# A 2-D FFT filter beside a gated MLP on one core: filter weights read in runs of four, the spectrum read from PSUM with a stride

## The chip, the cores and the metric

The kernel runs on one core of a Trainium2 chip. The metric is device time in microseconds (us) of one execution, measured outside the profiler. The profile of one execution stands beside it; its "span" runs from the first to the last instruction that it records. Engines are called TensorE (PE; its weight loads are PEld), VectorE (DVE), ScalarE (ACT), GpSimd (POOL) and SyncE (SP, which issues most of the DMAs here).

## What is computed

With x of 2048 x 640, in bf16:

```python
xn = layernorm(x)                              # over the 640 columns
X  = rfft2(xn); X = X * (w_r + 1j * w_i)       # 2048 x 321 complex filter
A  = irfft2(X)
B  = ((x_n @ w_gate) * (x_n @ w_up)) @ w_down  # 640 -> 1536 -> 640, x_n = xn
return x + A + B
```

All inputs and the output are bf16. The filter weights w_r and w_i are 2048 x 321 each.

## The kernel before, in words

The kernel is written as tasks (a few instructions of one engine each) with data dependencies, a duration that is written into the code, and a priority. A planner in the same file places the tasks on the engines by these durations before anything runs, and gives each engine one fixed list of instructions with its semaphore waits. So the order of the work follows from the tasks, their dependencies and the written durations, and not from what happens on the chip.

The stages overlap. First x is loaded, normalised and transposed (xn^T for the MLP). The 640 columns are split as 10 x 64: VectorE does the length-10 transforms by additions and multiplications (tasks S1 to S5, lines 833 to 873), TensorE the rest. The rows, 2048 = 32 x 64, are transformed in two matmul steps (R, line 884, and then D and C). The MLP's gate and up matmuls (GU, line 923; ten matmuls of 256 columns for most tasks) are scattered between all of this as filling for TensorE; ScalarE copies their results from PSUM (line 704), and VectorE multiplies gate and up (H, line 938).

The filter stage is a loop over 16 groups t of 128 spectrum rows each (line 947). One round has these tasks:

- four loads of filter weights into one of four buffers of `v_w` (line 698 by way of `dma`, each 64 rows x 321 columns, on SP's queue); a buffer is free when the multiplication four rounds earlier has read it.
- D (line 964): five matmuls finish the column transform; eD copies it from PSUM as bf16.
- C (lines 985 to 988): four matmuls of 321 columns make the real and imaginary spectrum in two neighbouring PSUM banks, 321 fp32 columns in each. The first 256 columns of a bank are four blocks k of 64 columns. Such a block holds two halves h of 32 columns m. Column (k, h, m) is frequency 10m + k + 1 for h = 0 and 10m + 9 - k for h = 1. The last 65 columns are the frequencies that are multiples of 5.
- WM (lines 992 to 1006): VectorE multiplies the spectrum in PSUM by the weights in SBUF. For each half h and each of w_r and w_i there is one TENSOR_TENSOR of 256 elements (line 1000), 2 banks x 4 k x 32 m with m innermost; then one of 260 elements for the last 65 columns (line 1003). The products are fp32 in `v_p`.
- CB (lines 1018 to 1022): four VectorE instructions add and subtract the products into the new real and imaginary parts, as bf16, in `v_y`; in `v_y` each block k holds three pieces of 64: the negated sum, the difference, the sum.
- NG (lines 1028 to 1030): ScalarE writes the negated sum (256 elements) and two small copies.
- IA (lines 1041 and 1042): ten matmuls, two for each of five blocks, go back along the rows; the 128 columns of a load of TensorE weights are two neighbouring pieces of `v_y`. eIA copies the result from PSUM.

After the 16 rounds come the inverse column transforms (I, line 1068, and V1 to V5 on VectorE), the accumulation with w_down (ACC, line 1141: 12 matmuls of 320 columns for each half of 128 output rows), one last matmul that adds A to it (line 1149), and the addition of x on VectorE (line 1156).

Of the kernel before, what the change touches and what calls it, by code (L numbers as in the profile page):

```python
# [495 lines left out]
_ACTF = mybir.ActivationFunctionType  # L496
_OP = AluOpType
# [13 lines left out]
def _d_mm(n):  # L511
    return max(n, 64) / 2.4 + 2.5
# [32 lines left out]
def _build(nc, A_x, A_w_r, A_w_i, B_w_gate, B_w_up, B_w_down, out, opts=None):  # L545
# [3 lines left out]
    with es:  # L549
# [68 lines left out]
        def V(name):  # L618
            off, sz = lay[name]
            return arena[:, off: off + sz]  # L620
# [8 lines left out]
        v_w = V("W").rearrange("p (r w l) -> p r w l", r=_NW, w=2)  # L629
# [5 lines left out]
        v_ti = V("TI").rearrange("p (t c n) -> p t c n", t=16, c=2)  # L635
# [14 lines left out]
        v_p = V("P").bitcast(_F32).rearrange("p (r w c l) -> p r w c l", r=2, w=2, c=2)  # L650
        v_y = V("Y").rearrange("p (r n) -> p r n", r=2)
# [37 lines left out]
        def bank_of(t):  # L689
            return t.units[1]  # L690
# [256 lines left out]
        for t in range(16):  # L947
            pq = 10.0 + 0.05 * t
            ar = t % 3
            r2 = t % 2  # L950
            wr = t % _NW
            for w_ in range(2):
                for h in range(2):
                    k2 = int(_rows(t, 0, h, 0))
                    dma("ld_w%d_%d_%d" % (t, w_, h), v_w[64 * h:64 * h + 64, wr, w_, 0:321], wvs[w_][:, k2, :],
                        64 * 642, [(b_w, ("r", 4 * wr + 2 * w_ + h, 4 * wr + 2 * w_ + h + 1))], prio=9.5 + 0.05 * t,
                        semkey=("w", wr), after=[wpad])

            def em_d(c, t=t):
                bk = bank_of(c.t)  # L960
                ins = None
                for k in range(5):
                    n = 128 if k < 4 else 130
                    ins = c.e.matmul(psflat[:, bk * 512 + k * 128: bk * 512 + k * 128 + n], v_uq[:, k, t, :],
                                     v_fd[:, k * 128: k * 128 + n], start=True, stop=True)
                return ins
            td = T("D_%d" % t, "pe", 5 * _d_mm(128), em_d, reads=[(b_u, None), (b_fd, None)],
                   prio=pq, bank="pair", cls="a")

            def em_ed(c, td=td, ar=ar):  # L970
                bk = bank_of(td)
                src = psflat[:, bk * 512: bk * 512 + 642]
                dst = v_a[:, ar, :].rearrange("p (c n) -> p c n", c=2)
                copy_on(c, dst[:, :, 0:256].rearrange("p c (k m) -> p k c m", k=4),
                        src[:, 0:512].rearrange("p (k c m) -> p k c m", k=4, c=2))
                return copy_on(c, dst[:, :, 256:321], src[:, 512:642].rearrange("p (c m) -> p c m", c=2))
            ed = T("eD_%d" % t, ("act", "dve"), {"dve": _d_dve_psum(512) + _d_dve_psum(130), "act": _d_act(512) + _d_act(130)}, em_ed,
                   writes=[(b_a, ("r", ar, ar + 1))], prio=pq - 0.001, frees=td)
            hold(td, ed)

            def em_c(c, t=t, ar=ar):
                bk = bank_of(c.t)
                a_r = v_a[:, ar, 0:_LP]
                a_i = v_a[:, ar, 324:324 + _LP]
                c.e.matmul(ps[:, bk, 0:_LP], v_tf[:, t, 0, :], a_r, start=True, stop=False)
                c.e.matmul(ps[:, bk + 1, 0:_LP], v_tf[:, t, 0, :], a_i, start=True, stop=False)
                c.e.matmul(ps[:, bk, 0:_LP], v_tf[:, t, 1, :], a_i, start=False, stop=True)
                return c.e.matmul(ps[:, bk + 1, 0:_LP], v_tf[:, t, 2, :], a_r, start=False, stop=True)
            tc = T("C_%d" % t, "pe", 4 * _d_mm(_LP), em_c, reads=[(b_a, ("r", ar, ar + 1)), (b_tf, ("t", t, t + 1))],
                   prio=pq, bank="pair", cls="a")  # L990

            def em_wm(c, tc=tc, r2=r2, wr=wr):
                bk = bank_of(tc)
                ins = None
                for h in range(2):
                    xh = ps[:, bk:bk + 2, 0:256].rearrange("p c (k h m) -> p h c k m", k=4, h=2)[:, h]
                    wv = v_w[:, wr, :, 0:320].rearrange("p w (m k) -> p w k m", k=10)
                    wv = wv[:, :, 1:5, :] if h == 0 else wv[:, :, 9:5:-1, :]
                    for w in range(2):
                        c.e.tensor_tensor(  # L1000
                            v_p[:, r2, w, :, 0:256].rearrange("p c (k h m) -> p h c k m", k=4, h=2)[:, h], xh,
                            wv[:, w].unsqueeze(1).to_broadcast([128, 2, 4, 32]), _OP.mult)
                ins = c.e.tensor_tensor(  # L1003
                    v_p[:, r2, :, :, 256:321], ps[:, bk:bk + 2, 256:321].unsqueeze(1).to_broadcast([128, 2, 2, 65]),
                    v_w[:, wr, :, 0:321:5].unsqueeze(2).to_broadcast([128, 2, 2, 65]), _OP.mult)
                return ins
            wm = T("WM_%d" % t, "dve", 4 * _d_dve_psum(256) + _d_dve_psum(260), em_wm,
                   reads=[(b_w, ("r", 4 * wr, 4 * wr + 4)), (b_wp, None)],
                   writes=[(b_p, ("r", r2, r2 + 1))], prio=pq - 0.001, frees=tc)
            hold(tc, wm)  # L1010

            def em_cb(c, r2=r2):
                p00, p01, p10, p11 = (v_p[:, r2, 0, 0], v_p[:, r2, 0, 1], v_p[:, r2, 1, 0], v_p[:, r2, 1, 1])

                def k4(v):
                    return v[:, 0:256].rearrange("p (k m) -> p k m", k=4)
                ym = v_y[:, r2, 0:768].rearrange("p (k s m) -> p k s m", k=4, s=3)
                c.e.tensor_tensor(ym[:, :, 2, :], k4(p01), k4(p10), _OP.add)  # L1018
                c.e.scalar_tensor_tensor(v_y[:, r2, 896:961], p01[:, 256:321], -1.0, p10[:, 256:321], _OP.mult,
                                         _OP.subtract)  # L1020
                c.e.tensor_tensor(v_y[:, r2, 768:833], p00[:, 256:321], p11[:, 256:321], _OP.subtract)
                return c.e.tensor_tensor(ym[:, :, 1, :], k4(p00), k4(p11), _OP.subtract)  # L1022
            T("CB_%d" % t, "dve", 2 * _d_dve(256) + 2 * _d_dve(65), em_cb,
              reads=[(b_p, ("r", r2, r2 + 1))], writes=[(b_y, ("r", 2 * r2, 2 * r2 + 1))], prio=pq - 0.001)

            def em_ng(c, r2=r2):
                ym = v_y[:, r2, 0:768].rearrange("p (k s m) -> p k s m", k=4, s=3)
                c.e.activation(ym[:, :, 0, :], ym[:, :, 2, :], _ACTF.Copy, scale=-1.0)  # L1028
                c.e.activation(v_y[:, r2, 833:896], v_y[:, r2, 897:960], _ACTF.Copy, scale=-1.0)
                return c.e.activation(v_y[:, r2, 961:1024], v_y[:, r2, 769:832], _ACTF.Copy)  # L1030
            T("NG_%d" % t, "act", _d_act(256) + 2 * _d_act(63), em_ng,
              reads=[(b_y, ("r", 2 * r2, 2 * r2 + 1))], writes=[(b_y, ("r", 2 * r2 + 1, 2 * r2 + 2))],
              prio=pq - 0.001)

            def em_ia(c, t=t, r2=r2):
                bk = bank_of(c.t)
                ins = None
                for k in range(5):
                    o1, o2 = (192 * k + 64, 192 * k) if k < 4 else (768, 896)
                    dst = psflat[:, bk * 512 + k * 128: bk * 512 + (k + 1) * 128]  # L1040
                    c.e.matmul(dst, v_y[:, r2, o1:o1 + 128], v_ti[:, t, 0, :], start=True, stop=False)  # L1041
                    ins = c.e.matmul(dst, v_y[:, r2, o2:o2 + 128], v_ti[:, t, 1, :], start=False, stop=True)  # L1042
                return ins
            ia = T("IA_%d" % t, "pe", 10 * _d_mm(128), em_ia, reads=[(b_y, ("r", 2 * r2, 2 * r2 + 2)), (b_ti, None)],
                   prio=pq, bank="pair", cls="a")

            def em_eia(c, ia=ia, t=t):
                bk = bank_of(ia)
                src = psflat[:, bk * 512: bk * 512 + 640].rearrange("p (k a m) -> p k a m", k=5, a=16)
                return copy_on(c, v_z2w[:, :, :, t, :], src)  # L1050
            eia = T("eIA_%d" % t, ("act", "dve"), {"dve": _d_dve_psum(640), "act": _d_act(640)}, em_eia,
                    writes=[(b_z2, ("t", t, t + 1))], prio=pq - 0.001, frees=ia)
            hold(ia, eia)
# [3 lines left out]
        for a in range(16):  # L1057
            pa = 19.0 + 0.05 * a
            pc = 41.0 + 0.05 * a
            r2 = a % 2  # L1060
# [185 lines left out]
```

## Time and profile before

| what | value |
|---|---|
| time, median of 3 runs (lowest to highest) | 224.96 us (224.48 to 225.21) |
| the profiled execution | 224.85 us |
| its span | 222.7 us |
| granted TensorE clock | 1.0 over the whole span |
| TensorE busy | 210.5 us, 2116 matmuls |
| VectorE busy | 197.7 us, 535 instructions |
| ScalarE busy | 129.4 us, 292 instructions |
| the 64 multiplications of line 1000 | 613 ns each, first start 89.3 us, last start 146.4 us |

A row of a group of instructions reads: line, engine, operation, what is written <- what is read, partitions x elements with type, xcount | busy time, mean ns of one | idle time of the engine just before them. Neighbouring rows of one engine overlap in the trace (an instruction is recorded until its last write, when the next has begun), so the time that an instruction takes in a full queue is read from start to start. In the rows of the timeline the columns are start, length, engine, line, operation, shape, count. In the rows of the waits they are who waited <- for whom: us in total, times, longest.

### The profile page before, as it was taken

The numbers are of one execution on the slowest core, as the hardware profiler recorded it, in microseconds if no ns is written. First come the engines' busy times: TensorE is split into PE (matmuls) and PEld (weight loads), VectorE is DVE, ScalarE is ACT, GpSimd is POOL, SyncE is SP. The second block draws the span as 40 slices with busy tenths as digits, with TensorE's granted clock in tenths as the row PEclk, the third lists the DMA queues.
The fourth block names the chain that finished last, engine by engine and source line by source line (L and its number), as shares of the span: only waits on it lengthen the run. The fifth ranks groups of instructions, "written<-read, shape, count | busy, mean of one in ns | idle before, by whom it ended". The sixth has DMA issues, their size and how long they took to land.

```text
span 222.7 us, 5325 instructions
## 1 busy us (share of the span) xinstructions
PE 210.5 (95%) x2116; PEld 173.0 (78%) x2116; DVE 197.7 (89%) x535; ACT 129.4 (58%) x292; POOL 0.2 (0%) x4
## 2 busy tenths in 40 slices
PE   8999999999999999889898989989999999999995
PEld 8989899988789988667676767779876767777773
DVE  3699999999999992999999999976999999999631
ACT  2575999999998658668677876587522012200000
POOL 0000000000000000000000000000000000000000
PEclk9999999999999999999999999999999999999999
DMA  7999990000000000012121211008622223332311
GB/s 196 306 345 393 405 204 9 0 3 0 1 3 0 3 0 3 21 40 53 39 49 44 52 41 30 3 0 258 215 60 61 74 72 93 92 99 78 116 46 44
DMA packets 22184, 19.78 MB, mean 89 GB/s; under 512 B 2192, under 2 KB 21264, under 8 KB 21904
## 3 DMA queue, kind: packets, MB, share of 16 engines
q1 hardware_dynamic: 20048, 18.37, 27.6%
q10 hardware_dynamic: 2112, 1.08, 1.9%
q8 instruction: 16, 0.26, 0.5%
q14 instruction: 8, 0.07, 0.1%
HBM read 16.82 MB, written 2.62 MB: 87 GB/s over the span
## 4 chain that ended last, share of the span: by engine, by line
PE 50%; DVE 42%; DMA 2%; ACT 2%; issue 1%; SPq 0%; DVEq 0%
PE ps L923 24%; PE ps L1141 20%; DVE arena L1000 14%; DVE arena L938 3%; DVE arena L1018 3%; DVE arena L1003 2%; DMA arena<-in_A_x_dram 2%; DVE arena L1022 2%; PE ps L1068 2%; ACT arena L704 2%; PE ps L1149 2%; PE ps L813 1%; PE ps L884 1%; DVE arena L798 1%; DVE arena L837 1%
## 5 line engine op out<-in xcount | busy, mean ns | idle before, releaser
L704 ACT ACTIVATE arena<-ps 128x512 bf16<-128x512 f32 (+5 forms) x200 | 106.6, 582 | 48.7 <-PE ps L1068 26.1
L923 PE MATMUL ps<-arena 128*128 128x256 bf16 (+1 forms) x1080 | 113.6, 261 | 3.3 <-DVE arena L1003 2.7
L923 PEld LDWEIGHTS ps<-arena 128*128 128x128 bf16 x1080 | 93.3, 98 | 14.7 <-DVE arena L1003 3.7
L1141 PE MATMUL ps<-arena 128*128 128x320 bf16 x384 | 56.7, 299 | 0.0
L1141 PEld LDWEIGHTS ps<-arena 128*128 128x128 bf16 x384 | 37.3, 98 | 14.2
L1000 DVE TENSOR_TENSOR arena<-ps,arena 128x256 f32<-128x256 f32 x64 | 35.0, 613 | 0.0
L938 DVE TENSOR_TENSOR arena<-arena 128x512 bf16<-128x512 bf16 (+1 forms) x54 | 20.9, 389 | 7.3 <-ACT arena L704 7.2
L1156 DVE TENSOR_TENSOR arena<-ps,arena 128x320 bf16<-128x320 f32 x32 | 15.5, 486 | 8.1 <-PE ps L1149 8.1
L1041 PE MATMUL ps<-arena 128*128 128x128 bf16 x80 | 10.7, 219 | 2.7 <-DVE arena L1003 1.9
L1041 PEld LDWEIGHTS ps<-arena 128*128 128x128 bf16 x80 | 7.6, 97 | 5.9 <-ACT arena L704 3.1
L1028 ACT ACTIVATE arena<-arena 128x256 bf16<-128x256 bf16 x16 | 6.6, 416 | 9.4 <-DVE arena L1022 9.4
L1042 PE MATMUL ps<-arena 128*128 128x128 bf16 x80 | 10.6, 219 | 0.0
L1149 PE MATMUL ps<-arena 128*128 128x320 bf16 x32 | 9.6, 299 | 0.0
L837 DVE TENSOR_TENSOR arena<-arena 128x384 f32<-128x384 bf16 x16 | 8.9, 554 | 0.0
L1042 PEld LDWEIGHTS ps<-arena 128*128 128x128 bf16 x80 | 7.8, 98 | 0.0
L764 DVE BATCH_NORM_STATS2 arena<-arena 128x6 f32<-128x320 bf16 x8 | 3.9, 490 | 3.8 <-DMA arena<-in_A_x_dram 3.6
L1003 DVE TENSOR_TENSOR arena<-ps,arena 128x260 f32<-128x260 f32 x16 | 7.1, 441 | 0.0
L1018 DVE TENSOR_TENSOR arena<-arena 128x256 bf16<-128x256 f32 x16 | 6.8, 425 | 0.2
L813 PE MATMUL ps<-arena 128*128 128x128 bf16 x80 | 6.3, 219 | 0.6 <-ACT arena L704 0.4
L757 ACT ACTIVATE arena<-arena 128x640 bf16<-128x640 bf16 x8 | 6.8, 846 | 0.0
L1022 DVE TENSOR_TENSOR arena<-arena 128x256 bf16<-128x256 f32 x16 | 6.8, 422 | 0.0
L838 DVE TENSOR_TENSOR arena<-arena 128x256 f32<-128x256 bf16 x16 | 6.7, 421 | 0.0
(71 smaller groups left out, 224.6 us busy)
## 6 DMA issues: line engine op xcount, KB each, us to landing
arena<-in_A_x_dram SPq DMA_DIRECT2D x20, 160.0 KB, 2.9
out_dram<-arena SPq DMA_DIRECT2D x32, 80.0 KB, 1.6
arena<-in_B_w_down_dram SPq DMA_DIRECT2D x1, 1920.0 KB, 9.0
arena<-c_tf SPq DMA_DIRECT2D x4, 384.0 KB, 11.6
arena<-in_A_w_r_dram SPq DMA_DIRECT2D x32, 40.1 KB, 2.3
arena<-in_A_w_i_dram SPq DMA_DIRECT2D x32, 40.1 KB, 2.3
arena<-in_B_w_gate_dram SPq DMA_DIRECT2D x4, 320.0 KB, 7.8
arena<-in_A_x_dram SPq DMA_DIRECT2D x1, 1280.0 KB, 12.1
```

The costliest lines, as they stand in the source:

```text
L704: return c.e.activation(dst, src, _ACTF.Copy)
L923: ins = c.e.matmul(ps[:, bk, w * n:(w + 1) * n], v_gw[:, w, j, ft, :], v_xt[:, j, rows], start=(j == 0), stop=(j == 4))
L938: return c.e.tensor_tensor(v_ht[:, ft0:ft0 + 2, rows], v_gbf[:, rr, :, 0:n], v_gbf[:, rr, :, n:2 * n], _OP.mult)
L1000: c.e.tensor_tensor(v_p[:, r2, w, :, 0:256].rearrange("p c (k h m) -> p h c k m", k=4, h=2)[:, h], xh, wv[:, w].unsqueeze(1).to_broadcast( ...
L1003: ins = c.e.tensor_tensor(v_p[:, r2, :, :, 256:321], ps[:, bk:bk + 2, 256:321].unsqueeze(1).to_broadcast([128, 2, 2, 65]), v_w[:, wr, :, 0 ...
L1018: c.e.tensor_tensor(ym[:, :, 2, :], k4(p01), k4(p10), _OP.add)
L1022: return c.e.tensor_tensor(ym[:, :, 1, :], k4(p00), k4(p11), _OP.subtract)
L1041: c.e.matmul(dst, v_y[:, r2, o1:o1 + 128], v_ti[:, t, 0, :], start=True, stop=False)
L1042: ins = c.e.matmul(dst, v_y[:, r2, o2:o2 + 128], v_ti[:, t, 1, :], start=False, stop=True)
L1141: ins = c.e.matmul(ps[:, bk, 0:320], v_ht[:, ft, a * 128:(a + 1) * 128], v_wd[:, ft, sl3], start=(ft == 0), stop=False)
L1149: return c.e.matmul(ps[:, bank_of(ag2), 0:320], v_sm[:, 2, :], v_v[:, a, sl3], start=False, stop=True)
L1156: return c.e.tensor_tensor(v_out[:, a % 2, sl3], ps[:, bk, 0:320], v_xr[:, xs, sl3], _OP.add)
```

## The change

Only access patterns change, in four tasks of the filter round. Each engine has the same instructions with the same numbers of elements in the same order with the same waits in both kernels; the durations written into the tasks are the same too.

- WM: the four multiplications of line 1000 run over 2 banks x 32 m x 4 k, with k innermost. The weights of one m are then four neighbours in SBUF (backwards for h = 1), and the next m is ten elements on. The spectrum in PSUM is read with k innermost, which is a step of 64 fp32 columns (256 bytes) from element to element. The products are written in order, for h = 0 in columns 0 to 127 and for h = 1 in columns 128 to 255, index 4m + k in each.
- CB and NG: the same sums in the new order, as one run of 256 elements each instead of four runs of 64. `v_y` holds the negated sum in 0 to 255, the difference in 256 to 511, the sum in 512 to 767.
- IA: for the first four blocks the 128 columns of the TensorE weights are taken from `v_y` with a step of four elements (8 bytes), where they were neighbours. The fifth block stays as it was.

```diff
                     xh = ps[:, bk:bk + 2, 0:256].rearrange("p c (k h m) -> p h c k m", k=4, h=2)[:, h]
-                    wv = v_w[:, wr, :, 0:320].rearrange("p w (m k) -> p w k m", k=10)
-                    wv = wv[:, :, 1:5, :] if h == 0 else wv[:, :, 9:5:-1, :]
+                    wv = v_w[:, wr, :, 0:320].rearrange("p w (m k) -> p w m k", k=10)
+                    wv = wv[:, :, :, 1:5] if h == 0 else wv[:, :, :, 9:5:-1]
                     for w in range(2):
                         c.e.tensor_tensor(
-                            v_p[:, r2, w, :, 0:256].rearrange("p c (k h m) -> p h c k m", k=4, h=2)[:, h], xh,
-                            wv[:, w].unsqueeze(1).to_broadcast([128, 2, 4, 32]), _OP.mult)
+                            v_p[:, r2, w, :, 128 * h:128 * h + 128].rearrange("p c (m k) -> p c m k", k=4),
+                            xh.rearrange("p c k m -> p c m k"), wv[:, w].unsqueeze(1).to_broadcast([128, 2, 32, 4]), _OP.mult)
...
-                ym = v_y[:, r2, 0:768].rearrange("p (k s m) -> p k s m", k=4, s=3)
-                c.e.tensor_tensor(ym[:, :, 2, :], k4(p01), k4(p10), _OP.add)
+                c.e.tensor_tensor(v_y[:, r2, 512:768], p01[:, 0:256], p10[:, 0:256], _OP.add)
...
-                return c.e.tensor_tensor(ym[:, :, 1, :], k4(p00), k4(p11), _OP.subtract)
+                return c.e.tensor_tensor(v_y[:, r2, 256:512], p00[:, 0:256], p11[:, 0:256], _OP.subtract)
...
-                c.e.activation(ym[:, :, 0, :], ym[:, :, 2, :], _ACTF.Copy, scale=-1.0)
+                c.e.activation(v_y[:, r2, 0:256], v_y[:, r2, 512:768], _ACTF.Copy, scale=-1.0)
...
                 for k in range(5):
-                    o1, o2 = (192 * k + 64, 192 * k) if k < 4 else (768, 896)
+                    if k < 4:
+                        l1, l2 = v_y[:, r2, 256 + k:768:4], v_y[:, r2, k:512:4]
+                    else:
+                        l1, l2 = v_y[:, r2, 768:896], v_y[:, r2, 896:1024]
                     dst = psflat[:, bk * 512 + k * 128: bk * 512 + (k + 1) * 128]
-                    c.e.matmul(dst, v_y[:, r2, o1:o1 + 128], v_ti[:, t, 0, :], start=True, stop=False)
-                    ins = c.e.matmul(dst, v_y[:, r2, o2:o2 + 128], v_ti[:, t, 1, :], start=False, stop=True)
+                    c.e.matmul(dst, l1, v_ti[:, t, 0, :], start=True, stop=False)
+                    ins = c.e.matmul(dst, l2, v_ti[:, t, 1, :], start=False, stop=True)
```

More of the change, by code (lines that the diff above doesn't have):

```diff
@@ L1013, in em_cb @@
                 p00, p01, p10, p11 = (v_p[:, r2, 0, 0], v_p[:, r2, 0, 1], v_p[:, r2, 1, 0], v_p[:, r2, 1, 1])
-                def k4(v):
-                    return v[:, 0:256].rearrange("p (k m) -> p k m", k=4)
-                ym = v_y[:, r2, 0:768].rearrange("p (k s m) -> p k s m", k=4, s=3)
-                c.e.tensor_tensor(ym[:, :, 2, :], k4(p01), k4(p10), _OP.add)
+                c.e.tensor_tensor(v_y[:, r2, 512:768], p01[:, 0:256], p10[:, 0:256], _OP.add)
                 c.e.scalar_tensor_tensor(v_y[:, r2, 896:961], p01[:, 256:321], -1.0, p10[:, 256:321], _OP.mult,
@@ L1026, in em_ng @@
             def em_ng(c, r2=r2):
-                ym = v_y[:, r2, 0:768].rearrange("p (k s m) -> p k s m", k=4, s=3)
-                c.e.activation(ym[:, :, 0, :], ym[:, :, 2, :], _ACTF.Copy, scale=-1.0)
+                c.e.activation(v_y[:, r2, 0:256], v_y[:, r2, 512:768], _ACTF.Copy, scale=-1.0)
                 c.e.activation(v_y[:, r2, 833:896], v_y[:, r2, 897:960], _ACTF.Copy, scale=-1.0)
```

## The prediction

> **What bounds the kernel now.** I read the page's busy shares first, then its chain, then the busy time in stages, then VectorE and TensorE row by row in one round of the filter stage.
>
> ```profile
> PE 210.5 (95%) x2116; PEld 173.0 (78%) x2116; DVE 197.7 (89%) x535; ACT 129.4 (58%) x292; POOL 0.2 (0%) x4
> PE 50%; DVE 42%; DMA 2%; ACT 2%; issue 1%; SPq 0%; DVEq 0%
> PE ps L923 24%; PE ps L1141 20%; DVE arena L1000 14%; DVE arena L938 3%; DVE arena L1018 3%; DVE arena L1003 2%; DMA arena<-in_A_x_dram 2%; DVE arena L1022 2%; PE ps L1068 2%; ACT arena L704 2%; PE ps L1149 2%; PE ps L813 1%; PE ps L884 1%; DVE arena L798 1%; DVE arena L837 1%
> ```
>
> Two engines share the chain, and the largest VectorE line in it is L1000, the multiplication that the change rewrites. The stage views say when VectorE is the one that binds: between 20 and 80 us, and between 89 and 149 us, where the 16 filter rounds run.
>
> ```profile
> core 0: us, PE busy (x) PEld busy (x) DVE busy (x) ACT busy (x) POOL busy (x), PEclk, DMA share, GB/s
> 20.00:80.00 60.00, 59.72 (x640) 52.65 (x639) 59.26 (x177) 53.94 (x115) 0.00 (x0) 1.00 0.23 73
> 89.00:149.00 60.00, 53.08 (x540) 42.05 (x539) 59.37 (x157) 42.92 (x113) 0.00 (x0) 1.00 0.16 34
> ```
>
> In the filter stage VectorE is busy 59.37 us of 60 and TensorE is idle for 60 - 53.08 = 6.9 us. ScalarE has 17 us to spare. From 20 to 80 us both engines are full, so two full engines can run side by side here. The waits in the stage agree, and all of them end at VectorE or at something that VectorE delayed:
>
> ```profile
> ACT arena L1028 <- DVE arena L1022: 9.4, 14, 1.5
> PEld ps L923 <- DVE arena L1003: 3.7, 6, 0.8
> PEld ps L1041 <- ACT arena L704: 3.1, 5, 0.6
> PE ps L923 <- DVE arena L1003: 2.7, 6, 0.6
> PE ps L1041 <- DVE arena L1003: 1.9, 5, 0.4
> ```
>
> One round on VectorE follows, with the columns start, length, line and count; it starts at 107.62 us, and the next begins at 111.35.
>
> ```profile
> 107.62 2.21 DVE L1000 TENSOR_TENSOR arena<-ps,arena 128x256 f32<-128x256 f32 x4
> 109.72 0.45 DVE L1003 TENSOR_TENSOR arena<-ps,arena 128x260 f32<-128x260 f32 x1
> 110.07 0.44 DVE L938 TENSOR_TENSOR arena<-arena 128x512 bf16<-128x512 bf16 x1
> 110.41 0.44 DVE L1018 TENSOR_TENSOR arena<-arena 128x256 bf16<-128x256 f32 x1
> 111.01 0.44 DVE L1022 TENSOR_TENSOR arena<-arena 128x256 bf16<-128x256 f32 x1
> 111.35 2.20 DVE L1000 TENSOR_TENSOR arena<-ps,arena 128x256 f32<-128x256 f32 x4
> ```
>
> A round is 3.73 us without a gap, and the four L1000 take 109.72 - 107.62 = 2.10 us of it, 0.525 us each from start to start.
>
> **The four multiplications.** Their price is out of line with their size:
>
> ```profile
> L1000 DVE TENSOR_TENSOR arena<-ps,arena 128x256 f32<-128x256 f32 x64 | 35.0, 613 | 0.0
> L1003 DVE TENSOR_TENSOR arena<-ps,arena 128x260 f32<-128x260 f32 x16 | 7.1, 441 | 0.0
> L837 DVE TENSOR_TENSOR arena<-arena 128x384 f32<-128x384 bf16 x16 | 8.9, 554 | 0.0
> L838 DVE TENSOR_TENSOR arena<-arena 128x256 f32<-128x256 bf16 x16 | 6.7, 421 | 0.0
> ```
>
> L837 and L838 differ by 128 elements and 133 ns, so 1.04 ns an element, and 421 - 256 x 1.04 = 155 ns fixed. L1003 reads PSUM in order and the weights in steps of five (10 bytes), and comes to (441 - 155) / 260 = 1.10 ns an element. L1000 reads PSUM in order too, but the weights in steps of ten (20 bytes): (613 - 155) / 256 = 1.79 ns. So the wide step over the weights costs about 0.7 ns an element, and PSUM as such nearly nothing. The Trainium skill (Vector Engine (DVE) Microarchitecture Reference, the part on the access granule under "Rate slope and fixed cost") gives 1.73 ns for one source that hops at every element; L1000's 1.79 agrees with it.
>
> The change reads the weights in runs of four neighbours (8 bytes, then the next run 20 bytes on). By L1003, where one element in 10 bytes is nearly free, four elements in 20 bytes are free. What replaces it is a PSUM read in which every element lies 64 floats (256 bytes) from the last. No row of this trace reads PSUM like that. The lower bound is no charge: L1003's price, 155 + 256 x 1.10 = 437 ns, or 178 ns less than now. A gain beyond that is excluded, since 1.04 ns is the rate of the rows that read everything in order. The nearest dear row is L1000 itself: if PSUM charges each jump as the weights are charged now, the price stays at 613 ns. The upper end that I take is a second element time for each element, 155 + 256 x 2.08 = 687 ns, 74 ns more than now. I take the lower value. Reason: TensorE writes PSUM in order at 128 elements in 56 ns (rows further down), more than twice the rate at which VectorE reads it, so that memory has speed to spare that a slot per element at 1.04 ns need not exhaust. That is a choice between rows, not a measurement, and the chances below show it.
>
> The Trainium skill speaks against the change here (Advanced Engine Details and Errata, "PSUM Cachelines"): lines of PSUM are 8 bytes, and "Every two consecutive elements should be contiguous for best throughput". It is said of matmuls; this trace shows no strided access of PSUM by any engine. Third rival.
>
> Sum on VectorE: 64 x 178 ns = 11.4 us. Durations overlap by about 90 ns from row to row (613 against 525), alike for a cheap row (L1003's 441 against 350), so the difference carries over. The four sums and negations lose their cut into four pieces (L1018 and L1022 cost 0.44 us, plain L838 421 ns): under 10 ns each, 32 of them, at most 0.3 us, taken as nothing. VectorE's work in the stage falls from 59.4 to 48.0 us.
>
> **What binds next.** TensorE then does. Its rows in one round give its own need from start to start:
>
> ```profile
> 104.11 0.30 PE L985 MATMUL ps<-arena 128*128 128x321 bf16 x1
> 104.66 0.44 PE L964 MATMUL ps<-arena 128*128 128x128 bf16 x5
> 104.94 1.26 PE L923 MATMUL ps<-arena 128*128 128x256 bf16 x10
> 106.57 0.22 PE L1041 MATMUL ps<-arena 128*128 128x128 bf16 x1 [0.38 <-DVE arena L1003]
> 106.63 0.22 PE L1042 MATMUL ps<-arena 128*128 128x128 bf16 x1
> 107.13 1.25 PE L923 MATMUL ps<-arena 128*128 128x256 bf16 x10
> 108.22 0.30 PE L985 MATMUL ps<-arena 128*128 128x321 bf16 x1
> ```
>
> The filter matmuls take 104.66 - 104.11 = 0.55 us, the transform before them 0.28, the ten inverse matmuls 107.13 - 106.57 = 0.56, ten gate matmuls 108.22 - 107.13 = 1.09. The stage holds
>
> ```profile
> 89.00:149.00 60.00, 32.46 (x266) 24.90 (x267) 1.00 0.16 34
> ```
>
> 266 gate matmuls (the row is of L923 alone), 26.6 x 1.09 = 29.0 us, and 16 x (0.55 + 0.28 + 0.56) = 22.2 us: 51.2 us. So the stage cannot go below 51, and VectorE's 48.0 is close behind. I add 1.8 us for waits that are left in the loop from VectorE over ScalarE's negation to the inverse matmuls (the stage from 20 to 80 us leaves 0.3, the stage now 6.9): 53.0 us, 7.0 us less. After 149 us TensorE runs full to 160 and the tail is bound by L1141's matmuls, neither touched; they move up as a block. The weight loads do not step in: 4 issues a round of 597 ns are 2.4 us of SP's queue, within a round of 3.3.
>
> ```profile
> L698 SPq DMA_DIRECT2D arena<-in_A_w_r_dram x32: 465/597/2201, 17.9 to 133.1; - x32
> ```
>
> No instruction or wait is added, and no engine's order changes, so nothing new can queue.
>
> **The strided matmul weights.** Of the ten inverse matmuls of a round eight now load their 128 columns 8 bytes apart.
>
> ```profile
> L1041 PEld LDWEIGHTS ps<-arena 128*128 128x128 bf16 x80 | 7.6, 97 | 5.9 <-ACT arena L704 3.1 <-ACT arena L1030 2.2 <-issue 0.3
> L1042 PEld LDWEIGHTS ps<-arena 128*128 128x128 bf16 x80 | 7.8, 98 | 0.0
> ```
>
> A load shows 98 ns, and yet matmuls start every 56 ns, so loads overlap. All loads of this trace read in order. Lower bound nothing (fewer than one load per matmul there cannot be). Upper bound by the row: loads that no longer overlap, 98 ns each, 8 x (98 - 56) = 0.34 us a round, 5.4 us in the stage. I take nothing: weights that stay in order load in half a matmul's latency, and eight loads are a tenth of a round. The Trainium skill (TensorE: Matmul & The Clock Gate, "Weight-path perf modes") says that the fast weight load covers packed and strided columns alike; no run here shows it yet. By that sentence the term is zero, by the row's bound 5.4 us.
>
> **The rivals.** *TensorE takes it back.* PSUM jumps are free, but strided loads are not: TensorE needs 51.2 + 5.4 = 56.6 us, with the same 1.8 us of waits 58.4, a gain of 1.6 us: 223.4, between 221 and 225. For it: TensorE has only 6.9 us in hand, so whatever its loads lose is lost from the gain. Against it: loads overlap so well today.
>
> *An even trade.* The step in PSUM costs what the step over the weights cost. L1000 stays near 613 ns, VectorE stays full, slower loads hide in TensorE's 6.9 us: 225.0, 223.5 to 227. For it: L1000 proves that VectorE pays for jumps on one side at least, and it may pay them whatever the memory.
>
> *The PSUM step is dearer, and the kernel slower.* At two element times each L1000 costs 74 ns more, 64 x 74 = 4.7 us, and VectorE, which is without a gap from 89 to 149 us, passes all of it on: 229.7. It decides from any price over 1.79 ns an element. A price of 2.5 ns would give 64 x 182 = 11.6 us more, 236.6; I hold that far end for unlikely. For it: the jump is 256 bytes instead of 20. Against it: the spare rate of PSUM named above.
>
> **How the numbers follow.** The profiled execution took 224.85 us, with 222.7 of span; the median of the runs is 224.96, 0.11 above, so differences carry over. My forecast, free jumps and unhurt loads, is 224.96 - 7.0 = 218.0 us, by itself 216 (no waits left, and some of the idle behind matmul ends recovered) to 220.5 (2.5 us more waits). Chances: forecast 0.37, TensorE takes it back 0.20, even trade 0.19, dearer 0.24. A measurement can tell 0.3%, 0.7 us, from no change. Faster: the forecast, 0.14 of the second, 0.02 of the third: 0.53. Same: 0.06 of the second and 0.08 of the third: 0.14. Slower: 0.09 of the third and the fourth: 0.33. The range of 8 in 10 runs from 216.5 to 230.0: it leaves out the far end of the last case and the edges of the first.
>
> **What would show it.** Right: L1000's rows near 437 ns, its four in 1.4 us, the span from the first to the last L1000 (89.3 to 146.4 us now) about 7 us shorter, TensorE's idle there below 2.5 us, waits on L1003 gone. LDWEIGHTS rows of the inverse matmuls still near 98 ns, and their ten matmuls still in 0.56 us. Wrong: L1000 at 600 ns or more; or L1000 cheap and the inverse matmuls at 0.9 us a round; or both as hoped and TensorE waiting on ScalarE's L1030 instead.

## The result, and the profile after

The kernel after takes 214.42 us (median of 4 runs, 214.31 to 215.54) beside 225.09 us for the kernel before in the same measurement: a ratio of the mean times of 0.9542, interval 0.9512 to 0.9572. That is 10.7 us less, where 7.0 was forecast, and below the range that was given.

The profiled execution of the kernel after is the slowest of its runs, 215.54 us with a span of 212.9; its filter stage begins 0.45 us later than before (86.81 us against 86.36 in the chains), ahead of anything that the change touches. That is part of why the spans differ by 9.8 us where the medians differ by 10.7.

The page's shares and the chain of the kernel after:

```profile
PE 206.6 (97%) x2116; PEld 174.0 (82%) x2116; DVE 185.9 (87%) x535; ACT 128.4 (60%) x292; POOL 0.2 (0%) x4
PE 74%; DVE 18%; DMA 4%; SPq 1%; issue 1%; ACT 1%; DVEq 0%
```

VectorE had 42% of the chain and has 18%; L1000 is gone from it. Its rows, the other rows of the round, and the loads of the inverse matmuls (line, engine, operation, shapes, count | busy us, mean ns | idle before):

```profile
L1000 DVE TENSOR_TENSOR arena<-ps,arena 128x256 f32<-128x256 f32 x64 | 22.6, 417 | 0.0
L1003 DVE TENSOR_TENSOR arena<-ps,arena 128x260 f32<-128x260 f32 x16 | 7.1, 442 | 0.0
L1015 DVE TENSOR_TENSOR arena<-arena 128x256 bf16<-128x256 f32 x16 | 6.8, 423 | 0.2
L1019 DVE TENSOR_TENSOR arena<-arena 128x256 bf16<-128x256 f32 x16 | 6.7, 419 | 0.0
L1040 PEld LDWEIGHTS ps<-arena 128*128 128x128 bf16 x80 | 8.8, 112 | 0.4
L1041 PEld LDWEIGHTS ps<-arena 128*128 128x128 bf16 x80 | 8.7, 113 | 0.1
```

The multiplication went from 613 to 417 ns, 1.02 ns an element over the fixed 155: the rate of rows that read everything in order, with a step of 256 bytes in PSUM. The sums hardly changed (425 to 423, 422 to 419 ns). The strided loads show 112 and 113 ns for 97 and 98, and each mean still contains the fifth block's loads, which are not strided; the strided ones alone show about 116 ns.

Now the stage. From the kernel before, the stretch from the first to the last multiplication (columns as in the views by stage: length, TensorE, its loads, VectorE, ScalarE, GpSimd, clock, DMA):

```profile
89.30:146.40 57.10, 50.18 (x514) 39.49 (x512) 56.86 (x151) 41.19 (x109) 0.00 (x0) 1.00 0.16 36
```

The same from the kernel after, and below it the whole of what stood between 89 and 149 us before, which is 49.8 us long now:

```profile
89.70:135.70 46.00, 45.42 (x501) 39.99 (x500) 45.26 (x151) 39.48 (x108) 0.00 (x0) 1.00 0.21 45
89.40:139.20 49.80, 49.22 (x541) 43.41 (x539) 47.69 (x157) 42.52 (x115) 0.00 (x0) 1.00 0.20 41
```

From the first to the last multiplication the stretch is 11.1 us shorter. VectorE was busy for 56.86 of 57.10 us and is busy for 45.26 of 46.00; TensorE had 6.9 us idle and has 0.6. By their busy time both engines are full; the experiments below say how much each has left. A round in the timeline of TensorE shows where its idle time was filled: ten inverse matmuls follow the gate matmuls without a gap, and this round, one of the longer ones, takes 3.57 us from one L985 to the next instead of 4.11 (104.11 to 108.22).

```profile
101.76 0.30 PE L985 MATMUL ps<-arena 128*128 128x321 bf16 x1
102.31 0.44 PE L964 MATMUL ps<-arena 128*128 128x128 bf16 x5
102.59 1.25 PE L923 MATMUL ps<-arena 128*128 128x256 bf16 x10
103.68 0.22 PE L1040 MATMUL ps<-arena 128*128 128x128 bf16 x1
104.24 1.25 PE L923 MATMUL ps<-arena 128*128 128x256 bf16 x10
105.33 0.30 PE L985 MATMUL ps<-arena 128*128 128x321 bf16 x1
105.88 0.22 PE L1040 MATMUL ps<-arena 128*128 128x128 bf16 x1
```

The ten inverse matmuls take 104.24 - 103.68 = 0.56 us, as before: strided loads cost nothing from start to start. The waits of the stage from 89 to 140 us in the kernel after follow. Those on L1003 are gone; ScalarE and VectorE wait, and TensorE only 0.6 us (its loads 0.8), for ScalarE's copies:

```profile
ACT arena L704 <- PE ps L923: 4.0, 10, 0.8
DVE arena L938 <- ACT arena L704: 2.8, 5, 1.4
ACT arena L704 <- PE ps L1041: 2.3, 5, 0.5
ACT arena L704 <- PE ps L964: 0.8, 1, 0.8
PEld ps L923 <- ACT arena L704: 0.8, 1, 0.8
PE ps L923 <- ACT arena L704: 0.6, 1, 0.6
```

The chain from 89 to 140 us, in which L1000 alone held 52.6% of the time from 89 to 149 us before, now lies on TensorE but for 1.6%:

```profile
by line: PE ps L923 58.1%; PE ps L1040 8.4%; PE ps L1041 8.3%; PE ps L964 6.6%; PE ps L988 4.3%; PE ps L987 4.3%; PE ps L986 4.3%; PE ps L985 4.2%; ACT arena L704 1.5%; issue 0.1%
```

After the stage the two kernels run alike: from the first inverse column matmul of the chain (L1068 at 169.67 us before, L1067 at 159.85 after) to the end both take 53.0 us.

### The profile page after: what moved, and what is told of

The parts are those of the page before. It is cut to its first block, busy times and chain, and to the rows that moved or that the text cites. A ratio compares the mean times of both kernels' runs of the same rounds, so it can differ in the third digit from the quotient of the medians.

```text
span 212.9 us, 5325 instructions
## 1 busy us (share of the span) xinstructions
PE 206.6 (97%) x2116; PEld 174.0 (82%) x2116; DVE 185.9 (87%) x535; ACT 128.4 (60%) x292; POOL 0.2 (0%) x4
## 4 chain that ended last, share of the span: by engine, by line
PE 74%; DVE 18%; DMA 4%; SPq 1%; issue 1%; ACT 1%; DVEq 0%
PE ps L923 36%; PE ps L1140 21%; DMA arena<-in_A_x_dram 4%; PE ps L1040 2%; PE ps L1041 2%; PE ps L1067 2%; PE ps L964 2%; DVE arena L938 2%; PE ps L1148 2%; PE ps L884 1%; DVE arena L837 1%; SPq L698 1%; PE ps L813 1%; DVE arena L798 1%; PE ps L985 1%; PE ps L988 1%
## 5 line engine op out<-in xcount | busy, mean ns | idle before, releaser
L923 PEld LDWEIGHTS ps<-arena 128*128 128x128 bf16 x1080 | 93.4, 98 | 11.4 <-ACT arena L704 1.9
L1140 PEld LDWEIGHTS ps<-arena 128*128 128x128 bf16 x384 | 37.2, 98 | 14.4 <-DMA arena<-in_B_w_down_dram 0.2
L1000 DVE TENSOR_TENSOR arena<-ps,arena 128x256 f32<-128x256 f32 x64 | 22.6, 417 | 0.0
L1041 PE MATMUL ps<-arena 128*128 128x128 bf16 x80 | 10.7, 219 | 0.0
L1040 PE MATMUL ps<-arena 128*128 128x128 bf16 x80 | 10.6, 219 | 0.0
L1040 PEld LDWEIGHTS ps<-arena 128*128 128x128 bf16 x80 | 8.8, 112 | 0.4
L1041 PEld LDWEIGHTS ps<-arena 128*128 128x128 bf16 x80 | 8.7, 113 | 0.1
L1003 DVE TENSOR_TENSOR arena<-ps,arena 128x260 f32<-128x260 f32 x16 | 7.1, 442 | 0.0
(71 smaller groups left out, 224.5 us busy)
## 6 DMA issues: line engine op xcount, KB each, us to landing
arena<-c_tf SPq DMA_DIRECT2D x4, 384.0 KB, 11.3
arena<-in_A_x_dram SPq DMA_DIRECT2D x1, 1280.0 KB, 11.3
```

What stands on the lines that cost most here:

```text
L923: ins = c.e.matmul(ps[:, bk, w * n:(w + 1) * n], v_gw[:, w, j, ft, :], v_xt[:, j, rows], start=(j == 0), stop=(j == 4))
L1000: c.e.tensor_tensor(v_p[:, r2, w, :, 128 * h:128 * h + 128].rearrange("p c (m k) -> p c m k", k=4), xh.rearrange("p c k m -> p c m k"), wv ...
L1003: ins = c.e.tensor_tensor(v_p[:, r2, :, :, 256:321], ps[:, bk:bk + 2, 256:321].unsqueeze(1).to_broadcast([128, 2, 2, 65]), v_w[:, wr, :, 0 ...
L1040: c.e.matmul(dst, l1, v_ti[:, t, 0, :], start=True, stop=False)
L1041: ins = c.e.matmul(dst, l2, v_ti[:, t, 1, :], start=False, stop=True)
L1140: ins = c.e.matmul(ps[:, bk, 0:320], v_ht[:, ft, a * 128:(a + 1) * 128], v_wd[:, ft, sl3], start=(ft == 0), stop=False)
```

## The experiments

The first theory was the prediction's, with the size corrected by the trace: the weights' step was the whole excess of the multiplication, the jumps in PSUM are free, and TensorE binds the stage now. Its rivals: something else in the change (the sums, the loads) made part of the gain; PSUM jumps cost something that is hidden; VectorE still sets the end.

Each comparison is with the kernel before, run on the same chip; its medians were 224.5 to 224.7 us in these runs. Where the text says how much more or less a run takes than the kernel after, it is against that kernel's 214.42 us; the ratios give the same differences within 0.3 us.

**Weights in runs of four, PSUM in order.**

```diff
-                    xh = ps[:, bk:bk + 2, 0:256].rearrange("p c (k h m) -> p h c k m", k=4, h=2)[:, h]
+                    xh = ps[:, bk:bk + 2, 128 * h:128 * h + 128].rearrange("p c (m k) -> p c k m", k=4)
```

> The kernel after, but the four multiplications read PSUM in order (128 neighbouring columns for each half) while the weights stay in runs of four. The spectrum columns meet other weights than they should: what is left out is the right pairing. Theory (the wide step over the weights was the whole excess, the jumps in PSUM are free): the multiplication stays at 417 ns, within 5, and the time at 214.4 us, within 0.6. Rival (PSUM jumps cost something that the change now pays): the multiplication falls to 400 ns or less; the time falls by up to 1 us, or not at all if TensorE binds.

Measured: 214.39 us (ratio 0.9543, 0.9494 to 0.9592), and

```profile
L1000 DVE TENSOR_TENSOR arena<-ps,arena x64: 411/416/425, 89.2 to 135.1; 128x256 f32<-128x256 f32 x64
```

a median of 416 ns, where the kernel after has 417. Taking the step in PSUM away gains nothing; beside weights in runs of four it is free.

**All of the change but the multiplications.** WM is as in the kernel before, CB, NG and IA as after:

```diff
-                    wv = v_w[:, wr, :, 0:320].rearrange("p w (m k) -> p w m k", k=10)
-                    wv = wv[:, :, :, 1:5] if h == 0 else wv[:, :, :, 9:5:-1]
+                    wv = v_w[:, wr, :, 0:320].rearrange("p w (m k) -> p w k m", k=10)
+                    wv = wv[:, :, 1:5, :] if h == 0 else wv[:, :, 9:5:-1, :]
...
-                            v_p[:, r2, w, :, 128 * h:128 * h + 128].rearrange("p c (m k) -> p c m k", k=4),
-                            xh.rearrange("p c k m -> p c m k"), wv[:, w].unsqueeze(1).to_broadcast([128, 2, 32, 4]), _OP.mult)
+                            v_p[:, r2, w, :, 0:256].rearrange("p c (k h m) -> p h c k m", k=4, h=2)[:, h], xh,
+                            wv[:, w].unsqueeze(1).to_broadcast([128, 2, 4, 32]), _OP.mult)
```

> The kernel after with only the multiplications undone: they read PSUM in order, step over the weights by 20 bytes and write as before; the sums and the negation in one run of 256 and the strided loads of the inverse matmuls stay, so the products are summed in the wrong order. Theory: the multiplication is back at 613 ns and the time at 225.0 us, within 0.7. Rival (part of the gain comes from the sums, the negation or the new loads): the time stays 1 us or more below 225.

Measured: 224.99 us (ratio 1.0013, 0.9993 to 1.0034), the multiplication back at 610 ns. The whole gain is the multiplications'; the sums and the strided loads alone change nothing that can be measured.

```profile
L1000 DVE TENSOR_TENSOR arena<-ps,arena x64: 595/610/648, 89.3 to 146.6; 128x256 f32<-128x256 f32 x64
```

**The loads in order again.**

```diff
-                        l1, l2 = v_y[:, r2, 256 + k:768:4], v_y[:, r2, k:512:4]
+                        l1, l2 = v_y[:, r2, 256 + 128 * k:384 + 128 * k], v_y[:, r2, 128 * k:128 * k + 128]
```

> The kernel after with only the loads of the inverse matmuls undone: 128 neighbouring columns each, which are other columns than the inverse needs. Theory (strided loads show 112 ns and not 98, but still hide behind the matmul in front): the rows are back at 98 ns and the time stays at 214.4 us, within 0.6. Rival (TensorE, which binds now, pays the 15 ns of each of 128 strided loads): 1.9 us less, 212.5.

Measured: 214.32 us (ratio 0.9531, 0.9493 to 0.9570), with the loads at 98 ns again. The 15 ns that a strided load shows are not paid by anyone, even where TensorE has no idle time.

```profile
L1040 PEld LDWEIGHTS ps<-arena 128*128 128x128 bf16 x80 | 7.8, 98 | 0.5
L1041 PEld LDWEIGHTS ps<-arena 128*128 128x128 bf16 x80 | 7.8, 98 | 0.2
```

**VectorE loaded again, by one and by two multiplications a round.** In the kernel after, behind the loop over h for one half, with a scratch buffer of its own (two of them in the second run):

```diff
+                    for w in range(1 if h == 0 else 0):
+                        c.e.tensor_tensor(
+                            v_sc[:, r2, w].rearrange("p c (m k) -> p c m k", k=4),
+                            xh.rearrange("p c k m -> p c m k"), wv[:, w].unsqueeze(1).to_broadcast([128, 2, 32, 4]), _OP.mult)
```

> The kernel after with a fifth multiplication like the other four in each round, into a scratch buffer: 16 x 0.33 = 5.3 us more for VectorE in the stage, no change elsewhere. Theory (TensorE binds the stage; VectorE is busy 49.0 us of its 54.7): the slack takes nearly all of it, at most 1.5 us more, 214.4 to 216. Rival (VectorE, or the loop through it, still sets the end): all of it, 219.7 us.

Measured: 218.24 us (ratio 0.9709, 0.9664 to 0.9755), 3.8 us more.

> The kernel after with two more multiplications like the other four in each round, into a scratch buffer: 10.6 us more for VectorE in the stage. Theory (VectorE has 5.7 us in hand there): it is full again, and the time rises by what goes beyond the slack, 4.5 to 6 us, to 219 to 220.5. Rival (VectorE still sets the end): 10.6 us more, 225.

Measured: 222.89 us (ratio 0.9929, 0.9913 to 0.9945), 8.5 us more. Both miss the theory and come nearer to its rival. The slack of 5.7 us that I had set was wrong: I had taken it from a stretch with the run-in and run-out of the stage. Between the first and the last multiplication VectorE has 0.74 us by its busy time, and with one more multiplication

```profile
89.10:139.30 50.20, 48.78 (x510) 39.51 (x508) 49.96 (x167) 40.92 (x109) 0.00 (x0) 1.00 0.20 41
```

that stretch is 4.2 us longer, with VectorE full and TensorE idle for 1.4; the chain from 89 to 140 us now lies on VectorE. The time says how much VectorE really had in hand: of 5.3 us it took up 5.3 - 3.8 = 1.5, and of 10.6 us 10.6 - 8.5 = 2.1. That is more than the 0.74 us that its busy time left.

**The same load in the kernel before.** One more of its own multiplications a round:

```diff
+                    for w in range(1 if h == 0 else 0):
+                        c.e.tensor_tensor(
+                            v_sc[:, r2, w].rearrange("p c (k m) -> p c k m", k=4),
+                            xh, wv[:, w].unsqueeze(1).to_broadcast([128, 2, 4, 32]), _OP.mult)
```

> The kernel before with a fifth multiplication of its own kind in each round, into a scratch buffer: 16 x 0.525 = 8.4 us more for VectorE. Theory (VectorE had no slack in the stage before): all of it is passed on, 233 to 233.6 us. Rival (some of the round was waiting that VectorE's rows don't show): 2 us or more below that.

Measured: 232.96 us (ratio 1.0372, 1.0354 to 1.0391), 8.4 us more than the kernel before beside it (224.54). Before the change VectorE passes on everything.

**TensorE lightened, after and before.** In both kernels the filter matmuls become

```diff
-                c.e.matmul(ps[:, bk, 0:_LP], v_tf[:, t, 0, :], a_r, start=True, stop=False)
-                c.e.matmul(ps[:, bk + 1, 0:_LP], v_tf[:, t, 0, :], a_i, start=True, stop=False)
-                c.e.matmul(ps[:, bk, 0:_LP], v_tf[:, t, 1, :], a_i, start=False, stop=True)
-                return c.e.matmul(ps[:, bk + 1, 0:_LP], v_tf[:, t, 2, :], a_r, start=False, stop=True)
+                c.e.matmul(ps[:, bk, 0:_LP], v_tf[:, t, 0, :], a_r, start=True, stop=True)
+                return c.e.matmul(ps[:, bk + 1, 0:_LP], v_tf[:, t, 0, :], a_i, start=True, stop=True)
```

> The kernel after with two of the four filter matmuls of each round left out (the cross terms of real and imaginary parts, so the spectrum is not the right one): 16 x 0.27 = 4.4 us less for TensorE in the stage. Theory (TensorE binds): the time falls by 3 to 4.4 us, to 210 to 211.4. Rival (VectorE or the loop through ScalarE binds): 214.4, no change.

> The kernel before with the same two matmuls of each round left out. Theory (VectorE binds the stage before, TensorE has idle time in it): 225.0 us, within 0.7. Rival (TensorE matters there too): 1 to 4.4 us less.

Measured: 212.94 us for the kernel after (ratio 0.9488, 0.9468 to 0.9508), 1.5 us less and not the 3 to 4.4 of the theory; 224.46 us for the kernel before (ratio 1.0007, 0.9995 to 1.0020), no change, as the theory had it. TensorE alone does not hold the stage after the change. With its 4.4 us gone VectorE is nearly full and TensorE idle for 1.2 us:

```profile
89.10:134.10 45.00, 43.83 (x469) 35.76 (x467) 44.76 (x150) 39.55 (x108) 0.00 (x0) 1.00 0.23 46
```

So the theory that TensorE binds now, with VectorE well clear of it, fell. The new one: in the rounds both engines are full, and either holds the end when the other is made lighter. Its rival was that VectorE alone holds it, and that TensorE's busy time is only stretched. Three more kernels tell these apart.

**VectorE lightened.** Only the two multiplications by w_r are made:

```diff
-                    for w in range(2):
+                    for w in range(1):
...
-                c.e.tensor_tensor(v_y[:, r2, 512:768], p01[:, 0:256], p10[:, 0:256], _OP.add)
+                c.e.tensor_tensor(v_y[:, r2, 512:768], p01[:, 0:256], p00[:, 0:256], _OP.add)
...
-                return c.e.tensor_tensor(v_y[:, r2, 256:512], p00[:, 0:256], p11[:, 0:256], _OP.subtract)
+                return c.e.tensor_tensor(v_y[:, r2, 256:512], p00[:, 0:256], p01[:, 0:256], _OP.subtract)
```

> The kernel after with two of the four multiplications of each round left out (those by w_i; the sums read the products by w_r twice): 16 x 2 x 0.33 = 10.6 us less for VectorE, TensorE unchanged. New theory (between the first and the last multiplication both engines are full after the change, VectorE 45.3 and TensorE 45.4 us of 46.0): TensorE holds the end, at most 1 us less, 213.4 to 214.4. Rival (VectorE alone sets the end, TensorE is only stretched busy): 5 us or more less, below 209.4.

Measured: 214.50 us (ratio 0.9547, 0.9532 to 0.9562). VectorE has 10 us of idle time in the rounds now, and nothing is gained:

```profile
89.40:134.50 45.10, 44.52 (x494) 39.58 (x493) 35.09 (x118) 38.54 (x105) 0.00 (x0) 1.00 0.22 46
```

**Both lightened,** by the last edit and the shorter filter matmuls together.

> The kernel after with both lightened: two of the four multiplications and two of the four filter matmuls of each round left out (10.6 us less for VectorE, 4.4 us less for TensorE). New theory (two full engines, either of which holds the end when the other is lightened alone): now the time falls by 3.5 to 4.4 us, to 210 to 211, though TensorE's 4.4 us alone gave 1.5. Rival (something third, ScalarE or the loop's latency, holds the stage): 212.5 or more.

Measured: 210.91 us (ratio 0.9392, 0.9378 to 0.9406), 3.5 us below the kernel after. TensorE's 4.4 us, worth 1.5 alone, are worth 3.5 when VectorE is out of the way, so in the run with TensorE lightened alone it was VectorE's work that held back the other 2.0.

**TensorE loaded.**

```diff
+                c.e.matmul(ps[:, bk, 0:_LP], v_tf[:, t, 1, :], a_i, start=True, stop=True)
+                c.e.matmul(ps[:, bk + 1, 0:_LP], v_tf[:, t, 2, :], a_r, start=True, stop=True)
                 c.e.matmul(ps[:, bk, 0:_LP], v_tf[:, t, 0, :], a_r, start=True, stop=False)
```

> The kernel after with two more filter matmuls in each round, whose results are overwritten: 16 x 0.27 = 4.4 us more for TensorE. New theory: all of it is passed on, 218 to 218.9 us. Rival (TensorE has slack in the stage): less than 2 us more.

Measured: 218.65 us (ratio 0.9735, 0.9719 to 0.9751), 4.2 us more: TensorE is full as well. The new theory holds in all three (the 214.50 us lie 0.1 above its range, less than the runs of that kernel differ among themselves), and its rival is refuted.

The two engines are not alike, though. TensorE holds the end, and VectorE comes about 1.5 us behind it. With these 1.5 us, read from the run with TensorE lightened, one more multiplication should cost 5.3 - 1.5 = 3.8 us (measured 3.8), two more 9.1 (8.5), VectorE lightened nothing (0.1 more), and both lightened 4.4 us less (3.5). What makes the 0.6 and 0.9 us that are off, no run shows.

**Both operands jump.** The weights again with 20 bytes from element to element, in another order than before:

```diff
-                    wv = v_w[:, wr, :, 0:320].rearrange("p w (m k) -> p w m k", k=10)
-                    wv = wv[:, :, :, 1:5] if h == 0 else wv[:, :, :, 9:5:-1]
+                    wv = v_w[:, wr, :, 1:289].rearrange("p w (m k) -> p w m k", k=9)[:, :, :, 0:1]
+                    wv = bass.AP(wv.tensor, wv.offset, [list(d) for d in wv.ap[:3]] + [[10, 4]])
```

> The kernel after, but the weights are read with 20 bytes from element to element again while the spectrum in PSUM is still read with its step of 256 bytes (the weights that the products get are the wrong ones). Theory (PSUM jumps are free, the weights' step costs 0.7 ns an element): 613 ns for the multiplication, as before, and 224 to 225.5 us. Rival (a jump in PSUM costs as well, but was hidden, since a run of four weights arrives with time to spare): 650 ns or more and 227 us or more.

Measured: 218.58 us (ratio 0.9737, 0.9710 to 0.9763), and the multiplication at

```profile
L1000 DVE TENSOR_TENSOR arena<-ps,arena 128x256 f32<-128x256 f32 x64 | 27.6, 494 | 0.0
```

494 ns, below both expectations. This run does not decide its question: its weights step 20 bytes three times and then 42 bytes back, over bytes next to those just read, and that order costs 1.32 ns an element and not 1.79. From the kernel after it differs in the order of the weights alone, so that order by itself is worth 77 ns beside PSUM jumps (417 to 494). The other 119 ns up to the old 613 were not taken apart: in the kernel before the multiplications also read PSUM and write their products in runs of 32 with gaps between, and no run changed the writing alone. The sums speak against it as a cause, since four runs of 64 cost them only 2 to 3 ns more than one run of 256. If the old price is all the weights', it belongs to the pattern of addresses and not to each jump. Whether a PSUM jump would add to a dear weight stream of the old pattern stays open; no run here had exactly that.

## Why the prediction was wrong, point by point

- **VectorE binds the stage before: right.** One more multiplication there cost 8.4 us of its own 8.4, and 4.4 us less on TensorE gained nothing.
- **The weights' step is the excess, and runs of four end it: right for the size of the gain, argued for the cause.** The multiplications are the whole gain, and the order of the weights alone was worth 77 of the 196 ns in one run; that it made the rest too, and not the writing in runs of 32, no run shows. At 417 ns the price is 20 below the forecast of 437: I had taken L1003's 1.10 ns an element and called a gain beyond that excluded, though 1.04 ns, the rate of the rows in order, gives 155 + 256 x 1.04 = 421. (The sum also has 178 ns where 613 - 437 is 176.) The Trainium skill's 1.73 ns for one source that hops at every element (Vector Engine (DVE) Microarchitecture Reference, the part on the access granule), given there for 4-byte words 4 KiB apart, fits L1000 before, at 1.79; the run with both operands jumping came to 1.32.
- **PSUM jumps free: right,** the choice between 437 and 687 ns. It was a choice, and in part luck: no run tests the reason given for it, the rate at which TensorE writes PSUM. The rule of 8-byte PSUM lines (Trainium skill, Advanced Engine Details and Errata, "PSUM Cachelines"), said of matmuls, does not carry over to a VectorE read of fp32 here: 417 ns with the step, 416 without. The even trade and the dearer step are refuted.
- **Strided loads nothing: right.** 214.32 us with the loads in order, 214.42 with the step. The sentence on fast weight loads of strided columns (Trainium skill, TensorE: Matmul & The Clock Gate, "Weight-path perf modes") agrees in that no time is lost, though the rows show 15 ns more, where the prediction had expected them to stay near 98. TensorE does not take the gain back.
- **Sums and negation nothing: right.** All of the change but the multiplications came to a ratio of 1.0013, with 1 inside its interval.
- **"So the stage cannot go below 51": the step that failed.** The sum put TensorE's need at 29.0 + 16 rounds x 1.39 = 51.2 us against a stretch of 60 us that does not hold 16 rounds of it. It holds all 16 rounds of VectorE's multiplications, but TensorE's part of a round runs ahead of them or behind. By 89 us two rounds of filter matmuls had started (88.09 and 88.64 us in TensorE's timeline), the second all but its last matmul, and the rows of that stretch hold 65 / 5 = 13 transforms, 14 filter groups and 75 / 5 = 15 inverse groups:

```profile
89.00:149.00 60.00, 5.58 (x65) 4.49 (x65) 1.00 0.16 34
89.00:149.00 60.00, 4.17 (x14) 1.34 (x14) 1.00 0.16 34
89.00:149.00 60.00, 10.03 (x75) 7.10 (x75) 1.00 0.16 34
```

(the rows of L964, L985 and L1041). That is 29.0 + 13 x 0.28 + 14 x 0.55 + 15 x 0.56 = 48.7 us, 2.5 less. The other term, 1.8 us of waits left over, was chosen between 0.3 and 6.9 with no row behind it; it came out as 49.8 - 48.7 = 1.1, of which the profile shows 0.6 as TensorE's idle time. So the stretch took 49.8 us where I had 53.0. These two, 2.5 + 0.7 = 3.2 us, are the gap between the forecast of 7.0 and the 10.2 us that the stretch became shorter.
- **"TensorE then does" bind: right, with VectorE closer behind than forecast.** TensorE passed on 4.2 of 4.4 us more, and VectorE lightened by 10.6 us gained nothing. But VectorE, which I had 3.2 us below TensorE (48.0 against 51.2), passed on 3.8 of 5.3 us more, so it was about 1.5 us below. With the two limits that close, the change gave nearly all that VectorE was relieved of: 56.86 - 45.26 = 11.6 us of busy time for 11.1 us of length.
- **The range** took its lower end, 216.5, from the miscounted floor; with 48.7 us the same steps give 60 - 48.7 - 1.8 = 9.5 us less, 215.5, and without the waits 11.3 less, 213.7.

## What to carry to other kernels

When an operation reads two operands and only one order can be regular, give the regular order to the operand whose row shows the excess: here the old order, with steady steps of 20 bytes over bf16 in SBUF, cost 0.7 ns an element more, and steps of 256 bytes over fp32 in PSUM cost nothing. A floor for the engine that binds next must be counted over exactly the stretch that it is compared with, group by group, since work that ran ahead of the stretch is not in it. Busy time can overstate how full an engine is: VectorE was busy for all but 0.74 us of the rounds and still took up 1.5 us of more work. And when two engines are both nearly full, lightening either one alone gains little (0 and 1.5 us here) and lightening both gains what neither showed (3.5 us).

## What the runs showed of the hardware that was not expected

- A VectorE read of fp32 in PSUM with 256 bytes from element to element runs at the rate of an in-order read: 417 against 416 ns for 256 elements.
- Multiplications whose bf16 weights have a steady step of 20 bytes cost 1.79 ns an element (613 ns, beside products written in runs of 32), with three steps of 20 bytes and one of 42 bytes back 1.32 ns (494 ns, beside PSUM jumps), in runs of four neighbours every 20 bytes 1.02 ns (417 ns).
- TensorE weights taken 8 bytes apart show loads of about 116 ns instead of 98 (112 to 113 in the rows, where one load in five is in order), and their matmuls still start every 56 ns.
